# Scores of a pair of heads: two products of 64 rows instead of one block-diagonal product of 128

## The chip, the cores and the metric

One Trainium2 chip, one core. The metric is device time in microseconds of one execution of the whole kernel; lower is better. Every time here comes from runs on the chip, or from the profile of one execution (page, trace).

## The reference

Inputs: q, k, v of 8 batches, 8 heads, 576 positions, 64 values per head; weights of a gated unit. Keys and values are pooled by 8 along the sequence, so each head has 72 pooled keys.

```python
k_p = k.reshape(B, H, Sp, pool, D).mean(axis=3)          # Sp = 576 / 8 = 72
v_p = v.reshape(B, H, Sp, pool, D).mean(axis=3)
scores = scale * np.matmul(q, k_p.transpose(0, 1, 3, 2)) # (B, H, 576, 72)
scores = scores - np.max(scores, axis=-1, keepdims=True)
attn = np.exp(scores)
attn = attn / (np.sum(attn, axis=-1, keepdims=True) + 1e-09)
x = np.matmul(attn, v_p)                                 # then (B, 576, 512)
h = gelu(x @ w_in); u, v = h[..., :512], h[..., 512:]    # tanh form of gelu
v_n = layernorm(v) * g_ln
v_s = np.einsum('ts,bsd->btd', w_sg, v_n) + b_sg[None, :, None]
out = x + (u * v_s) @ w_out
```

All of it is float32. The change is in the line of `scores`.

## The kernel before

The eight heads of a batch are worked on as four pairs (G = 4). For each batch and pair there are small steps, each a Python generator that gives way at its `yield`s: A, B, C and E load k, v, q and what is left over; K pools the keys and puts them into `kbd`; P prepares the pooled values; Q transposes q into `qT`; S computes scores and the softmax; L and T turn the softmax so that keys lie on partitions; V multiplies with the values; H, U, W and O are the products of the gated unit; X and Z finish and store.

The order of all work is written out by hand: the list `PROLOGUE` names one step and batch per word (`S0+3` is the next piece of step S, pair 0, batch 3), and `emit` runs through it. At the end every instruction is tied to the one before it on its engine (line 908), so each engine's order is fixed by that list; only the waits between engines move in time. Engines meet through the tile framework's semaphores.

`mm` (line 138) issues every matrix product, so all of them have line 139 in the profile; the names of tiles tell them apart. Most products use operands split into a high and a low part of type F32R; the scores use plain float32 operands, and such a product appears in the trace as two weight loads and two matmuls.

`kbd` (line 164) holds the pooled keys of all pairs: 128 partitions, 4 pairs, 144 columns. Partitions 0 to 63 are the 64 values of the even head, partitions 64 to 127 those of the odd head. Step K writes the even head's 72 keys into columns 0 to 71 of the upper 64 partitions, and the odd head's into columns 72 to 143 of the lower 64; the other two blocks are zero from the memset in line 165. So one product of `qT` (128 partitions: both heads' values; 576 positions) with `kbd` gives both heads' scores side by side: 144 columns, half of the multiplications being with zeros.

Step S (lines 532 to 583) does that for five blocks of 128 positions (NT = 5; the last block overlaps the one before). `qT`'s block is the operand loaded into the array, `kbd` the one that is streamed. Scores go into one PSUM tile of two banks of 512 values (`mtile()` for batch 0, `atile()` after that, both in rings of two). Blocks stand SLOT = 184 values apart in the flat tile, so three blocks lie in the first bank and two in the second. After a `yield`, VectorE finds the negated maximum of each position and head in one instruction over all five blocks (`nmax`, line 545); ScalarE then runs ten exponentials, one per block and head, each with its own maximum as bias and its sum as a second output (line 564); VectorE adds 1e-9 (line 571), writes the reciprocal, for most steps into two unused PSUM values behind each block (line 577), and scales `e` (line 223). GpSimd copies the last 16 columns aside (line 583).

The tile `aps` is also used by steps L, T (in the first two batches) and V, and the pooling by TensorE in the first two batches (`kvraw` with `ident`, line 390).

Of the kernel before, what the change touches and what calls it, by code (L numbers as in the profile page):

```python
# [13 lines left out]
AF = mybir.ActivationFunctionType  # L14
ALU = mybir.AluOpType
AX = mybir.AxisListType

P = 128
# [75 lines left out]
def tile_pooled_attn_gmlp(ctx: ExitStack, tc: tile.TileContext, q, k, v, w_in, g_ln, w_sg, b_sg, w_out, out):  # L94
    nc = tc.nc
    B, H, S, D = q.shape
    DM = w_in.shape[0]
    DF2 = w_in.shape[1] // 2
    SP = S // POOL
# [3 lines left out]
    NT = -(-S // P)  # L103
    TAIL = S - (NT - 1) * P
    HALF = S // 2
    NB = 512
    SLOT = 184
    NATURAL = (0,)
    FINE = (B - 1,)
    BY_PSUM = ("v",)  # L110
# [16 lines left out]
    def ring(pool, shape, name, bufs):  # L127

        turns[name] = (turns.get(name, -1) + 1) % bufs
        return pool.tile(shape, F32, name=name, tag=f"{name}{turns[name]}")  # L130

    def mtile():
        return ring(psm, [P, 2, NB], "mps", 2)

    def atile():
        return ring(psa, [P, 2, NB], "aps", 2)

    def mm(o, lhsT, rhs, start, stop):
        nc.tensor.matmul(o, lhsT, rhs, start=start, stop=stop)  # L139
# [24 lines left out]
    kbd = const.tile([P, G, 2 * SP], F32, name="kbd")  # L164
# [39 lines left out]
    def ready(func):  # L204

        if loaded.get("now") != func:
            nc.scalar.activation(early, eps[:, 0:1], func)  # L207
        loaded["now"] = func
# [13 lines left out]
    def scale(o, x, y, key):  # L222
        (nc.gpsimd if key in OTHER else nc.vector).tensor_tensor(o, x, y, op=ALU.mult)  # L223
# [307 lines left out]

    def step_S(b, g):
        qT = st.pop(("qT", b, g))
        flat = (mtile() if b == 0 else atile()).rearrange("p a n -> p (a n)")
        slots = []
        for i in range(NT):
            o = flat[:, SLOT * i:SLOT * i + 2 * SP]

            t0 = min(i * P, S - P)
            mm(o, qT[:, t0:t0 + P], kbd[:, g], True, True)  # L540
            slots.append(o.rearrange("p (h k) -> p h k", h=2))
        yield
        nmax = per.tile([P, NT, 2], F32, name="nmax", tag=f"nmax{g}")
        every = flat[:, 0:SLOT * NT].rearrange("p (s k) -> p s k", k=SLOT)[:, :, 0:2 * SP]
        nc.vector.tensor_reduce(out=nmax, in_=every.rearrange("p s (h k) -> p s h k", h=2),  # L545
                                axis=AX.X, op=ALU.max, negate=True)
        yield

        e = ring(per, [P, NT, 2, SP], "e", 3)
        ssum = per.tile([P, NT, 2], F32, name="ssum", tag=f"ssum{g}")  # L550
        mode = SOFTMAX.get(b, 0)
        if mode == 2:

            scores = every.rearrange("p s (h k) -> p s h k", h=2)
            nc.vector.tensor_tensor(e, scores, nmax.unsqueeze(3).broadcast_to([P, NT, 2, SP]), op=ALU.add)
            yield
            ready(AF.Exp)
            nc.scalar.activation(e, e, AF.Exp)
        else:
            ready(AF.Exp)  # L560
            for i in range(NT):
                for h in range(2):
                    acc = {} if mode else {"accum_out": ssum[:, i, h:h + 1]}
                    nc.scalar.activation(e[:, i, h], slots[i][:, h], AF.Exp, bias=nmax[:, i, h:h + 1], **acc)  # L564
        if mode:
            yield
            nc.vector.tensor_reduce(out=ssum, in_=e, axis=AX.X, op=ALU.add)
            nc.vector.tensor_scalar(ssum, ssum, 1e-9, None, op0=ALU.add)
        else:
            yield  # L570
            nc.vector.tensor_tensor(ssum, ssum, eps[:, 0:1].unsqueeze(2).broadcast_to([P, NT, 2]), op=ALU.add)

        key = f"n{min(b, 2)}{g}"
        rec = flat[:, 0:SLOT * NT].rearrange("p (s k) -> p s k", k=SLOT)[:, :, 2 * SP:2 * SP + 2]
        if key in OTHER:
            rec = ssum
        nc.vector.reciprocal(rec, ssum)
        scale(e, e, rec.unsqueeze(3).broadcast_to([P, NT, 2, SP]), key)
        ef = st["e", b, g] = e.rearrange("p t h k -> p t (h k)")
        yield  # L580
        if ("el", b) not in st:
            st["el", b] = per.tile([P, NT, 2, NL, 2], F32, name="el")
        nc.gpsimd.tensor_copy(st["el", b][:, :, g // 2, :, g % 2], ef[:, :, P:2 * SP])
# [274 lines left out]
    def step_Z(b, m):  # L858
        if b in FINE:
# [10 lines left out]


    steps = {"A": step_A, "B": step_B, "C": step_C, "E": step_E, "K": step_K, "P": step_P, "Q": step_Q, "S": step_S, "L": step_L, "T": step_T, "V": step_V,
             "H": step_H, "U": step_U, "W": step_W, "O": step_O, "X": step_X, "Z": step_Z}
    going = {}
# [60 lines left out]
```

## Time and profile before

| | us |
|---|---|
| median of 3 runs | 561.77 (561.52 to 562.21) |
| the profiled execution | 560.36 |
| its span (first to last instruction) | 558.7 |
| TensorE, matmuls busy | 538.1 (96%) |
| TensorE, weight loads busy | 508.7 (91%) |
| VectorE busy | 435.2 (78%) |
| ScalarE busy | 330.6 (59%) |
| GpSimd busy | 260.8 (47%) |

In the profile PE is TensorE's matmuls and PEld its weight loads, which overlap the matmuls; DVE is VectorE, ACT ScalarE, POOL GpSimd, SP the engine that issues most DMAs. A tile is named without its number in the ring. A group of instructions stands as line, engine, operation, output <- inputs, shapes, count, then busy time in us and the mean of one in ns, then the idle time before it and what ended it. For TensorE a shape such as 128*64 is rows by columns of the array. A matmul's record includes its way through the array, so records of products that follow closely overlap one another: what a product costs in a stream is the distance between two starts, and not its length.

### The profile page before, as it was taken

How to read it: one execution, taken by the hardware profiler on the slowest of the kernel's cores; microseconds unless marked ns; L12 is line 12 of the kernel's file. 1: busy time of each engine (PE TensorE's matmuls, PEld its weight loads, DVE VectorE, ACT ScalarE, POOL GpSimd, SP SyncE). 2: the span in 40 equal slices, each digit the busy share in tenths (PEclk: the TensorE clock that was granted, in tenths of full speed). 3: DMA queues.
4: the chain of work that ended last, by engine and by line, in shares of the span. 5: the costliest groups of instructions: out<-in, count | busy, mean ns of one | idle time of the engine just before them, and what ended most of it. 6: DMA issues, size and time to landing. Idle time of an engine off the chain costs nothing.

```text
span 558.7 us, 10694 instructions
## 1 busy us (share of the span) xinstructions
PE 538.1 (96%) x3677; PEld 508.7 (91%) x3677; DVE 435.2 (78%) x644; ACT 330.6 (59%) x1077; POOL 260.8 (47%) x322
## 2 busy tenths in 40 slices
PE   5799998999999999999999999999999999999997
PEld 4687987999999989999999989999999989998996
DVE  2899999998879979788888788788667798736254
ACT  3899995695348924587358834696338674322210
POOL 4365648843815254455507356533707243344130
PEclk9999999999999999999999999999999999999999
DMA  8996342365654365645747377517564423230206
GB/s 246 315 298 164 93 120 76 69 145 122 158 147 90 93 155 146 138 111 134 166 104 158 86 177 162 119 48 151 122 169 99 95 44 83 78 59 2 32 13 106
DMA packets 186470, 68.38 MB, mean 122 GB/s; under 512 B 150576, under 2 KB 170800, under 8 KB 186416
## 3 DMA queue, kind: packets, MB, share of 16 engines
q1 hardware_dynamic: 182560, 67.11, 49.9%
q10 hardware_dynamic: 3856, 0.59, 0.6%
q8 instruction: 29, 0.48, 0.3%
q14 instruction: 25, 0.20, 0.1%
HBM read 48.20 MB, written 19.46 MB: 121 GB/s over the span
## 4 chain that ended last, share of the span: by engine, by line
PE 78%; DVE 9%; ACT 4%; SPq 3%; DMA 3%; issue 1%; POOL 0%; DVEq 0%; ACTq 0%; POOLq 0%
PE mps L139 66%; PE aps L139 12%; SPq L240 3%; ACT e L564 2%; DMA kvraw<-in_k 1%; ACT L207 1%; DVE vg L739 1%; DVE bst L733 1%; DVE al L649 0%; DMA al<-tfar 0%; DVE top L237 0%; DMA lfar<-y 0%; DVE e L223 0%; DVE raw L228 0%; DVE wsl L320 0%
## 5 line engine op out<-in xcount | busy, mean ns | idle before, releaser
L564 ACT ACTIVATE e<-aps,nmax 128x72 f32<-128x72 f32 x280 | 85.0, 354 | 6.3 <-DVE nmax L545 6.2
L139 PE MATMUL mps<-xhl,wih 128*128 128x288 f32 x512 | 88.2, 294 | 0.0
L139 PE MATMUL mps<-wih,xhl 128*128 128x512 f32 x256 | 84.7, 396 | 0.6 <-DVE wsl L320 0.3
L139 PEld LDWEIGHTS mps<-xhl,wih 128*128 128x128 f32 x512 | 75.5, 188 | 1.0
L237 POOL TENSOR_TENSOR glo<-u,ghi 128x576 fp32r<-128x576 f32 x29 | 42.4, 1478 | 69.9 <-ACT ghi L214 35.5
L564 ACT ACTIVATION_READ_ACCUMULATOR e<-aps,nmax 128x1 f32 x280 | 67.4, 242 | 0.0
L237 POOL TENSOR_TENSOR xhl<-x,xhl 128x576 fp32r<-128x576 f32 x30 | 43.8, 1471 | 41.9 <-ACT xhl L692 37.6
L139 PEld LDWEIGHTS mps<-wih,xhl 128*128 128x128 f32 x256 | 48.1, 188 | 11.1 <-ACT u L771 0.7
L139 PE MATMUL mps<-wsh,vhl 128*128 128x288 f32 x256 | 55.1, 296 | 0.3 <-DVE vhl L237 0.3
L139 PE MATMUL mps<-xhl,wil 128*128 128x288 f32 x256 | 54.8, 295 | 0.0
L139 PE MATMUL mps<-wsl,vhh 128*128 128x288 f32 x256 | 54.8, 295 | 0.0
L139 PE MATMUL mps<-wsh,vhh 128*128 128x288 f32 x256 | 54.7, 295 | 0.0
L139 PE MATMUL mps<-ghi,woh 128*128 128x288 f32 (+1 forms) x232 | 51.8, 302 | 0.0
L139 PE MATMUL mps<-ghi,wol 128*128 128x288 f32 (+1 forms) x232 | 50.8, 298 | 0.0
L139 PE MATMUL mps<-glo,woh 128*128 128x288 f32 (+1 forms) x232 | 50.8, 298 | 0.0
L139 PE MATMUL mps<-wil,xhl 128*128 128x512 f32 x128 | 50.1, 391 | 0.0
L785 DVE SCALAR_TENSOR_TENSOR mps<-mps,gcol,bbc 128x576 f32<-128x576 f32 x32 | 26.2, 819 | 27.6 <-PE mps L139 27.6
L237 POOL TENSOR_TENSOR vhl<-vg,vhh 128x512 fp32r<-128x512 f32 x25 | 34.6, 1389 | 23.5 <-DVE vhh L212 18.6
L736 POOL TENSOR_TENSOR rstd<-mv,eps 128x1 f32<-128x1 f32 (+1 forms) x40 | 13.0, 325 | 68.8 <-DVE mv L734 65.5
L646 ACT CAST ah<-al 128x640 fp32r<-128x640 f32 x24 | 17.5, 731 | 41.6 <-DMA al<-tfar 37.9
L139 PEld LDWEIGHTS mps<-wsh,vhl 128*128 128x128 f32 x256 | 41.1, 188 | 0.6 <-DVE vhl L237 0.6
L139 PEld LDWEIGHTS mps<-wsh,vhh 128*128 128x128 f32 x256 | 41.2, 188 | 0.0
(210 smaller groups left out, 1428.8 us busy)
## 6 DMA issues: line engine op xcount, KB each, us to landing
kvraw<-in_k SPq DMA_DIRECT2D x16, 512.0 KB, 4.3
kvraw<-in_v SPq DMA_DIRECT2D x16, 512.0 KB, 4.3
qraw<-in_q SPq DMA_DIRECT2D x112, 72.0 KB, 2.6
out<-y SPq DMA_DIRECT2D x112, 72.0 KB, 2.1
tfar<-y SPq DMA_DIRECT2D x24, 320.0 KB, 2.5
al<-tfar SPq DMA_DIRECT2D x96, 80.0 KB, 2.2
raw<-in_moe_w_in SPq DMA_DIRECT2D x4, 1024.0 KB, 7.8
y<-lfar SPq DMA_DIRECT2D x36, 80.0 KB, 2.1
```

What stands on the lines that cost most here:

```text
L139: nc.tensor.matmul(o, lhsT, rhs, start=start, stop=stop)
L207: nc.scalar.activation(early, eps[:, 0:1], func)
L237: (nc.vector if key in OTHER else nc.gpsimd).tensor_tensor(o, x, y, op=op)
L240: queue.dma_start(o, i)
L564: nc.scalar.activation(e[:, i, h], slots[i][:, h], AF.Exp, bias=nmax[:, i, h:h + 1], **acc)
L646: nc.scalar.copy(ah, al)
L733: nc.vector.bn_stats(bst, vg)
L736: nc.gpsimd.tensor_tensor(rstd, mv[:, 1:2], eps[:n, 1:2], op=ALU.add)
L739: nc.vector.scalar_tensor_tensor(vg, vg, mv[:, 0:1], rstd.broadcast_to([n, DF2]), op0=ALU.subtract, op1=ALU.mult)
L785: nc.vector.scalar_tensor_tensor(vs, vs, gcol[:, d:d + 1], bbc.rearrange("p (a n) -> p a n", a=2), op0=ALU.mult, op1=ALU.add)
```

## The change

The five products of a step become ten. For each block of positions and each of the two heads `h`, the product takes only that head's 64 partitions of `qT` and `kbd` and that head's 72 columns. The even head's scores go into the first bank of the tile, the odd head's into the second; within a bank the five blocks stand SLOT = 96 values apart. The maximum, the exponentials and the reciprocal read and write the same number of values at the new places; the reciprocal now stands in one unused value behind each block and head. `kbd` is filled as before; its zero blocks are no longer read.

```diff
-    SLOT = 184
+    SLOT = 96
...
     def step_S(b, g):
         qT = st.pop(("qT", b, g))
-        flat = (mtile() if b == 0 else atile()).rearrange("p a n -> p (a n)")
-        slots = []
+        slots = (mtile() if b == 0 else atile())[:, :, 0:SLOT * NT].rearrange("p h (s k) -> p s h k", k=SLOT)
         for i in range(NT):
-            o = flat[:, SLOT * i:SLOT * i + 2 * SP]
             t0 = min(i * P, S - P)
-            mm(o, qT[:, t0:t0 + P], kbd[:, g], True, True)
-            slots.append(o.rearrange("p (h k) -> p h k", h=2))
+            for h in range(2):
+                r = slice(D * h, D * h + D)
+                mm(slots[:, i, h, 0:SP], qT[r, t0:t0 + P], kbd[r, g, SP * h:SP * h + SP], True, True)
         yield
         nmax = per.tile([P, NT, 2], F32, name="nmax", tag=f"nmax{g}")
-        every = flat[:, 0:SLOT * NT].rearrange("p (s k) -> p s k", k=SLOT)[:, :, 0:2 * SP]
-        nc.vector.tensor_reduce(out=nmax, in_=every.rearrange("p s (h k) -> p s h k", h=2),
-                                axis=AX.X, op=ALU.max, negate=True)
+        nc.vector.tensor_reduce(out=nmax, in_=slots[:, :, :, 0:SP], axis=AX.X, op=ALU.max, negate=True)
...
-                    nc.scalar.activation(e[:, i, h], slots[i][:, h], AF.Exp, bias=nmax[:, i, h:h + 1], **acc)
+                    nc.scalar.activation(e[:, i, h], slots[:, i, h, 0:SP], AF.Exp, bias=nmax[:, i, h:h + 1], **acc)
...
-        rec = flat[:, 0:SLOT * NT].rearrange("p (s k) -> p s k", k=SLOT)[:, :, 2 * SP:2 * SP + 2]
+        rec = slots[:, :, :, SP]
         if key in OTHER:
             rec = ssum
```

More of the change, by code (lines that the diff above doesn't have):

```diff
@@ L552, in step_S @@
         if mode == 2:
-            scores = every.rearrange("p s (h k) -> p s h k", h=2)
-            nc.vector.tensor_tensor(e, scores, nmax.unsqueeze(3).broadcast_to([P, NT, 2, SP]), op=ALU.add)
+            nc.vector.tensor_tensor(e, slots[:, :, :, 0:SP], nmax.unsqueeze(3).broadcast_to([P, NT, 2, SP]), op=ALU.add)
             yield
```

## The prediction

> **What bounds the kernel now.** I read the page first: the span, the busy shares and the chain that ended last.
>
> ```profile
> span 558.7 us, 10694 instructions
> PE 538.1 (96%) x3677; PEld 508.7 (91%) x3677; DVE 435.2 (78%) x644; ACT 330.6 (59%) x1077; POOL 260.8 (47%) x322
> PE 78%; DVE 9%; ACT 4%; SPq 3%; DMA 3%; issue 1%; POOL 0%; DVEq 0%; ACTq 0%; POOLq 0%
> ```
>
> TensorE is busy 96% of the span and holds 78% of the chain. An average can hide stages, so next comes the view by stretches (stretch, its length, busy time of PE, PEld, DVE, ACT and POOL with their instructions, then clock and DMA):
>
> ```profile
> 0.00:50.00 50.00, 38.68 (x257) 33.80 (x258) 36.66 (x56) 36.78 (x130) 24.62 (x43) 1.00 0.90 259
> 50.00:100.00 50.00, 46.77 (x316) 42.99 (x315) 47.52 (x75) 40.84 (x133) 35.00 (x41) 1.00 0.39 109
> 100.00:200.00 100.00, 100.00 (x700) 96.24 (x699) 87.44 (x131) 66.47 (x240) 48.08 (x60) 1.00 0.52 119
> 300.00:400.00 100.00, 98.96 (x666) 93.37 (x665) 81.03 (x124) 65.55 (x235) 53.11 (x66) 1.00 0.54 122
> 450.00:540.00 90.00, 89.11 (x604) 84.14 (x603) 53.85 (x80) 31.79 (x68) 34.62 (x40) 1.00 0.21 46
> ```
>
> From 100 us on TensorE is never without work, and its clock is granted in full. What it waited for from 100 us to the end is one short list:
>
> ```profile
> PE aps L139 <- DVE e L223: 1.0, 1, 1.0
> PE mps L139 <- POOL xta L218: 0.4, 1, 0.4
> PE mps L139 <- DVE vhl L237: 0.3, 1, 0.3
> ```
>
> So time that a product saves or costs on TensorE after 100 us goes to the end nearly one to one. The products that change are those of step S, scores from the tiles qT and kbd. The view of tile qT (matmuls, count, shortest/median/longest ns, first and last start) and its busy time by stretch (the first number after the length) say how many there are and where:
>
> ```profile
> L139 PE MATMUL aps<-kbd,qT x280: 283/286/390, 48.4 to 446.8; 128*128 128x144 f32 x140
> L139 PE MATMUL mps<-kbd,qT x40: 286/286/390, 14.3 to 26.6; 128*128 128x144 f32 x40
> 50.00:100.00 50.00, 4.24 (x30) 1.00 0.39 109
> 100.00:200.00 100.00, 10.61 (x80) 1.00 0.52 119
> 200.00:300.00 100.00, 7.90 (x60) 1.00 0.61 145
> 300.00:400.00 100.00, 8.41 (x61) 1.00 0.54 122
> 400.00:450.00 50.00, 5.65 (x40) 1.00 0.50 114
> ```
>
> Each of the 32 steps issues 5 products, and an f32 product stands as two records, each with its own weight load: 10 loads and 10 matmuls a step, 320 in all. About 240 of them, 24 steps, lie after 100 us. The chain of waits (start, length, what) runs through them:
>
> ```profile
> 106.85 2.45 PE aps L139 x20
> 181.41 1.23 PE aps L139 x10
> 185.01 1.22 PE aps L139 x10
> 244.16 1.23 PE aps L139 x10
> ```
>
> One step costs 1.225 us of the path; two back to back cost 2.45. That is 0.1225 us a record.
>
> **The change, part by part.** *Removed:* 10 pairs of load and matmul per step (128 rows, 128 weight columns, 144 moving columns), 1.225 us. *Added:* 20 pairs per step, each of 64 rows, 128 weight columns and 72 moving columns; those of the even head stand in rows 0 to 63 and write one half of the tile (one PSUM bank), those of the odd head in rows 64 to 127 and the other half. What a pair costs has two parts.
>
> The matmul: if time goes by moving columns, 72 of them cost 0.1225 x 72/144 = 0.061 us. The load: it still has 128 columns. Two places price it. In the first, weights of 64 and of 128 columns follow each other after a wait, by the timeline of loads (start, length):
>
> ```profile
> 461.20 0.13 PEld L139 LDWEIGHTS mps<-wil,xta 128*64 128x64 f32 x1 [0.90 <-POOL xta L218]
> 461.25 0.19 PEld L139 LDWEIGHTS mps<-wih,xta 128*128 128x128 f32 x1
> 461.49 0.14 PEld L139 LDWEIGHTS mps<-wil,xta 128*64 128x64 f32 x1
> 461.72 0.19 PEld L139 LDWEIGHTS mps<-wih,xta 128*128 128x128 f32 x1
> ```
>
> The second load begins 0.05 us behind the first: 64 columns occupy the load path for about 0.05 us, and as the records' means differ by 0.054 us, too (below), 128 columns occupy it for about 0.108. In the second place, pairs with 128 moving columns, the pooling of k and v, run back to back:
>
> ```profile
> L139 PEld LDWEIGHTS mps<-wil,xta 128*64 128x64 f32 x32 | 4.3, 134 | 2.4 <-POOL xta L218 0.9
> L139 PEld LDWEIGHTS mps<-xhl,wih 128*128 128x128 f32 x512 | 75.5, 188 | 1.0
> L139 PEld LDWEIGHTS aps<-lt,vl 96*128 96x128 f32 x48 | 9.1, 189 | 0.0
> 60.85 1.95 PE L139 MATMUL aps<-kvraw,ident 128*128 128x128 f32 x16
> ```
>
> Sixteen starts in 1.95 us less the last record's 0.29: 1.66/15 = 0.111 us a pair. So a load of 128 columns costs 0.108 to 0.111 us, and 96 rows cost what 128 rows cost (189 and 188 ns): halving the rows makes no load cheaper. Now the load, not the matmul, sets the pace of a pair (0.111 against 0.061).
>
> Hence the question that decides the sign: do loads of the two row groups run side by side? No row of this trace has 64 rows, so both bounds stand. Side by side, each group passes 10 loads: 10 x 0.111 = 1.11 us a step, a gain of 0.115. One behind the other: 20 x 0.111 = 2.22 us, a loss of 0.99. I take side by side: the rows show that a load's time goes by columns and not by rows, as it would where each row of the array takes in its own weights, and loads here already run under matmuls in flight. That is the nearer reading, not a proof.
>
> The Trainium skill bears on this on both sides. In "TensorE: Matmul & The Clock Gate", section LDWEIGHTS, a load costs its column count whatever its rows; the trace agrees (188 and 189 ns), and by this rule alone, with one load at a time, the change doubles the load time. In "TensorEngine Tiling (Array Packing)", Key Properties, tiles load weights and multiply in parallel; no run here shows it yet.
>
> *Switching the array* between products of 128 rows and of 64: the nearest rows are products of 64 weight columns between those of 128, matmuls on the same timeline:
>
> ```profile
> 461.49 0.39 PE L139 MATMUL mps<-wih,xta 128*128 128x512 f32 x1
> 461.72 0.39 PE L139 MATMUL mps<-wil,xta 128*64 128x512 f32 x1
> 461.95 0.40 PE L139 MATMUL mps<-wih,xta 128*128 128x512 f32 x1
> ```
>
> They follow each other every 0.23 us, less than a record's own 0.39, so nothing drains between the two shapes. I take nothing for a switch; the upper bound is a full drain: the flight of the last product (0.286 - 0.122 = 0.164) and an uncovered load (0.108), 0.27 us, at each way in and out.
>
> The same page of the Trainium skill, Key Properties, says that changing the tiling mode drains the engine; the rows above speak against it for columns, and rows are not tried here. It is a rival below.
>
> *Readers of the scores:* the maximum, the exponentials and the reciprocal keep their counts and sizes.
>
> ```profile
> L545 DVE TENSOR_REDUCE nmax<-aps 128x10 f32<-128x720 f32 x28 | 25.0, 894 | 11.3 <-PE aps L139 11.2
> L564 ACT ACTIVATE e<-aps,nmax 128x72 f32<-128x72 f32 x280 | 85.0, 354 | 6.3 <-DVE nmax L545 6.2
> L577 DVE RECIPROCAL aps<-ssum 128x10 f32<-128x10 f32 x28 | 6.3, 224 | 1.0
> ```
>
> Only strides change; the old layout also had three products in one bank and two in the other. I cost this at nothing: VectorE and ScalarE have slack under TensorE (87 and 66 of 100 us). Without that cover even a tenth on the 894 ns would be 28 x 0.09 = 2.5 us. No wait, DMA or queue entry is added or moved; the next step behind S on TensorE starts earlier or later by what S gains or loses.
>
> **The sum.** 24 steps x (1.11 - 1.225) = -2.8 us. Of the 8 steps before 100 us, where the stretches show TensorE with idle time, 0 to 8 x -0.115 = -0.9; I take -0.3. Together -3.1. The profiled execution took 560.36 us with a span of 558.7; its sum is 557.3. The median of the runs is 561.77, 1.4 above it, so the forecast for the median is **558.7 us**.
>
> **The rivals.**
> *Loads one behind the other* (slower). Place: the load path in step S. Price: 24 x 0.99 = +23.7, and 0 to +7.9 for the early eight, of which I take +3: about 588.5 us, bounds 585.5 to 593.4. It decides once the mean spacing of S's loads is above 0.061 us, where 20 of them exceed 1.225. For it: loads on TensorE stand in one order, and every f32 product needs two. Against it: that rows don't enter a load's time.
> *A drain at each switch.* The steps after 100 us come in about 18 stretches, since pairs like that at 106.85 share one: 18 x 2 x 0.27 = +9.7 on top of -3.1, 568.4 us; with a third of that price it would end where it began. Against it: the 64-column rows.
> *The change doesn't do what it says.* Loads overlap but the matmuls of the two groups take turns: 20 x 0.061 = 1.22 us a step, as before: 561.7 us.
> *Both faster.* If loads, too, were paced below the 0.061 of a matmul, a step would take 0.61 us: 24 x -0.61 = -14.7, 547 us. The 0.108 speaks against it.
> *Loads in turn and a drain:* 598 us.
>
> **How the numbers follow.** Forecast 0.37, both faster 0.04, no gain 0.10, drain 0.14, loads in turn 0.32, in turn with a drain 0.03. A measurement of this kernel can tell about 0.2% (1.1 us) from no change. Faster: 0.37 + 0.04 = 0.41. Same: 0.10 and 0.02 of the drain's (a small one that eats the gain) = 0.12. Slower: 0.12 + 0.32 + 0.03 = 0.47. The forecast's own range is 557 to 560.5 us, from the 0.108 and 0.111 and the early steps. As cases of both signs hold most of the chance, the range runs from 556.5 to 591: it leaves out the faster extreme, loads in turn with a drain, and the upper third of the loads in turn.
>
> **What would show it.** In the profile after, the records of qT and kbd have 64 rows and 72 columns and are twice as many (640). Right: the chain's piece for one step is about 1.11 us, loads of both groups begin within some ns of each other, and the product after S follows without a gap. Loads in turn: those starts are 0.108 us apart and the piece is 2.2 us. A drain: some 0.2 us of idle TensorE before the first load of S and behind the last matmul. The forecast is wrong if a step's piece is above 1.2 us, or if TensorE shows new waits for DVE or ACT behind S.

## The result, and the profile after

The changed kernel takes 569.52 us (median of 4 runs, 566.21 to 570.59) against 561.99 for the kernel before (561.52 to 563.04). The ratio is 1.0118, with a 95% interval from 1.0096 to 1.0141: slower by 1.2% (7.5 us between the medians). The forecast was 558.7 us, so its sign was wrong; the time lies inside the range given. The profiled execution took 569.15 us with a span of 567.4, 8.8 us above the profiled one of before.

The page after: span, busy shares, the granted clock in 40 slices and the engines of the chain.

```profile
span 567.4 us, 11333 instructions
PE 546.8 (96%) x3997; PEld 511.6 (90%) x3997; DVE 436.1 (77%) x644; ACT 331.1 (58%) x1077; POOL 260.1 (46%) x322
PEclk9699999999999999999999999999999999999999
PE 74%; DVE 12%; DMA 5%; ACT 3%; SPq 3%; issue 2%; POOL 0%; DVEq 0%; ACTq 0%; POOLq 0%
```

There are 320 more loads and matmuls, VectorE and ScalarE are as busy as before, and the clock falls to 0.6 in the second slice (14 to 28 us), which it did not do before. Where the time goes is read best from the view of tile qT, whose first and last starts can be set beside those in the prediction:

```profile
L139 PE MATMUL aps<-kbd,qT x560: 272/272/327, 52.8 to 455.6; 64*128 64x72 f32 x187
L139 PE MATMUL mps<-kbd,qT x80: 272/280/486, 15.8 to 30.9; 64*128 64x72 f32 x80
```

The steps of batch 0 (`mps`) began at 14.3 us before and begin at 15.8; the first step after them began at 48.4 and begins at 52.8, 4.4 us late; the last one began at 446.8 and begins at 455.6, 8.8 us late. The end is 8.7 us late. So half of the loss is there before 53 us, half comes in the 400 us of steps, and after the last step nothing is added.

Of the first 4.4 us, 1.5 are a later start. Ahead of the first step ScalarE waits for a load from memory, before and then after:

```profile
10.55 1.16 ACT L285 ACTIVATE mps<-raw 128x512 f32<-128x512 f32 x2 [2.01 <-DMA raw<-in_moe_w_in]
```

```profile
12.08 1.16 ACT L285 ACTIVATE mps<-raw 128x512 f32<-128x512 f32 x2 [3.25 <-DMA raw<-in_moe_w_in]
```

No instruction that the change touches stands ahead of it. In the traces of the experiments below this wait is 1.9 to 3.3 us, and in the kernel before and its versions alone 2.0 to 3.1 us. So these 1.5 us are more likely scatter than a part of the change, though that isn't proved.

The second half first. Matmuls (the first three lines) and weight loads (the last four) around two adjacent steps after the change; start, length:

```profile
110.89 0.42 PE L139 MATMUL mps<-wtl,vht 128*128 128x288 f32 x2
111.24 2.46 PE L139 MATMUL aps<-kbd,qT 64*128 64x72 f32 x40
113.62 0.53 PE L139 MATMUL mps<-wsh,vhh 128*128 128x288 f32 x2
...
110.76 0.32 PEld L139 LDWEIGHTS mps<-wtl,vht 128*128 128x128 f32 x2
111.24 0.19 PEld L139 LDWEIGHTS aps<-kbd,qT 64*128 64x128 f32 x2 [0.16 <-issue]
111.24 2.31 PEld L139 LDWEIGHTS aps<-kbd,qT 64*128 64x128 f32 x40 [0.16 <-issue]
113.62 0.30 PEld L139 LDWEIGHTS mps<-wsh,vhh 128*128 128x128 f32 x2
```

The same stretch in the kernel before:

```profile
106.42 0.43 PE L139 MATMUL mps<-wtl,vht 128*128 128x288 f32 x2
106.68 2.61 PE L139 MATMUL aps<-kbd,qT 128*128 128x144 f32 x20
109.04 0.52 PE L139 MATMUL mps<-wsh,vhh 128*128 128x288 f32 x2
...
106.55 2.53 PEld L139 LDWEIGHTS aps<-kbd,qT 128*128 128x128 f32 x20
109.01 0.31 PEld L139 LDWEIGHTS mps<-wsh,vhh 128*128 128x128 f32 x2
```

Three things are to be seen. *The row groups do run side by side:* two loads begin within 111.24 to 111.25 us (the row with x2 is that window), and 40 loads in 2.31 - 0.19 us are 20 pairs, 2.12/19 = 0.112 us a pair. A step costs 1.12 us instead of 1.225, as forecast. *On the way in there is a gap:* before, the loads of S began at 106.55, under the last product of W (which ended at 106.85); after, they begin at 111.24, only 0.07 us ahead of that product's end at 111.31, and TensorE's loads stand still for 0.16 us. *On the way out, too:* from the end of S (111.24 + 2.46 = 113.70) to the end of the next two matmuls (114.15) pass 0.45 us, where it was 0.27 (109.29 to 109.56): 0.18 us more; the loss of a single step by starts, below, gives 0.20.

The chain shows the way in and the steps together, for a pair of steps and for a single one:

```profile
111.31 2.38 PE aps L139 x40
250.05 1.27 PE aps L139 x20
```

A single step is 1.27 = 1.12 + 0.15, and 0.20 on the way out: 1.47 against 1.225, a loss of 0.24. A pair is 2.38 + 0.20 = 2.58 against 2.45, a loss of 0.13. The 24 steps after 100 us stand in 12 single stretches and 6 pairs: 12 x 0.24 + 6 x 0.13 = 3.7 us by these prices. Read stretch by stretch, as the shift between the two traces from the products ahead of a stretch to those behind it, it is 3.0 us: the six pairs lose 0.12 to 0.13 each and nine of the single steps 0.23 to 0.25, but the other three, whose first load came late in the kernel before, too, hardly anything (-0.07 to 0.09). The rest of the 4.4 us that the tile's starts show, about 1.4, comes between the stretches, in part as short waits of TensorE that are longer in this trace (for `vhl` 0.7 us instead of 0.3). Why they are longer was not followed.

What is left of the first half, some 2.9 us, goes with the clock. Busy time by stretch, 9 to 36 us, before and then after (after the five engines: granted clock, DMA):

```profile
9.00:36.00 27.00, 21.21 (x164) 18.93 (x164) 22.68 (x38) 22.61 (x104) 9.64 (x14) 1.00 1.06 319
```

```profile
9.00:36.00 27.00, 21.18 (x173) 19.32 (x172) 18.46 (x32) 18.46 (x95) 6.92 (x9) 0.81 1.02 313
```

In these 27 us TensorE was granted 0.81 of its clock after the change, and all of it before. Cut where the clock changes, the trace after shows full clock and half clock in turn (the second and the fourth line are at 0.50):

```profile
9.62:16.42 6.80, 3.17 (x32) 2.67 (x32) 3.55 (x6) 3.19 (x9) 0.52 (x2) 1.00 0.92 228
16.44:19.84 3.40, 3.40 (x24) 3.04 (x20) 2.27 (x4) 1.60 (x9) 1.26 (x1) 0.50 1.13 324
19.86:23.25 3.39, 2.10 (x26) 1.72 (x25) 3.02 (x6) 3.39 (x22) 2.17 (x2) 1.00 1.04 394
23.27:30.08 6.81, 6.45 (x40) 6.12 (x42) 5.32 (x10) 6.26 (x37) 1.87 (x3) 0.50 1.05 308
```

In all four runs of the change the mean clock over the whole span is 0.987 to 0.992.

### The profile page after: what moved, and what is told of

Read it like the earlier page. It is cut to its first block, busy times and chain, and to the rows that moved or that the text cites. A ratio compares the mean times of both kernels' runs of the same rounds, so it can differ in the third digit from the quotient of the medians.

```text
span 567.4 us, 11333 instructions
## 1 busy us (share of the span) xinstructions
PE 546.8 (96%) x3997; PEld 511.6 (90%) x3997; DVE 436.1 (77%) x644; ACT 331.1 (58%) x1077; POOL 260.1 (46%) x322
## 4 chain that ended last, share of the span: by engine, by line
PE 74%; DVE 12%; DMA 5%; ACT 3%; SPq 3%; issue 2%; POOL 0%; DVEq 0%; ACTq 0%; POOLq 0%
PE mps L139 60%; PE aps L139 13%; SPq L240 3%; DMA raw<-in_moe_w_in 1%; DMA al<-tfar 1%; DVE vg L735 1%; DVE e L223 1%; DVE bst L729 1%; ACT e L560 1%; DMA out<-y 1%; DVE al L645 1%; DVE ssum L567 1%; DMA lfar<-y 0%; DVE y L863 0%; DVE top L288 0%
```

## The experiments

The first four take the loss apart by place and by switch. Batch 0 back in the old form:

```diff
...
         for i in range(NT):
 
             t0 = min(i * P, S - P)
+            if b == 0:
+                mm(slots[:, i], qT[:, t0:t0 + P], kbd[:, g].rearrange("p (h k) -> p h k", h=2), True, True)
+                continue
             for h in range(2):
...
```

(The lines left out give batch 0 its old places in PSUM, 184 values apart.)

> The change everywhere but in batch 0, whose four steps keep the one product of 128 rows. Theory: half of the 7.5 us comes from the first 35 us, where the granted clock fell to 0.5 for some 10 us in the profile after, and half from 0.15 us on the way into 64 rows and 0.20 us on the way out of them at each of the later stretches. Then the clock stays at 1.00 and 565.5 to 567 us remain. Rival, the early loss has nothing to do with the batch-0 products (a late load, or the program's greater length): about 569.5 us, clock 0.99. Rival, the later stretches cost nothing: 562 us.

Measured: 564.71 us (1.0052 of before, 1.0036 to 1.0068), clock 0.997 to 1.000 in four runs. Its steps in the view by tile:

```profile
L139 PE MATMUL aps<-kbd,qT x560: 272/272/327, 48.6 to 451.2; 64*128 64x72 f32 x187
L139 PE MATMUL mps<-kbd,qT x40: 286/286/390, 14.4 to 26.7; 128*128 128x144 f32 x40
```

The first step after batch 0 is back at 48.6 us, the last is 4.4 us late. The early loss is gone and the later one is whole. The time is 0.8 us below the expected band, and 2.8 us above the kernel before; between the runs of both with a clock of 0.999 or more it is 3.2 us.

The opposite, the new form in batch 0 alone (the same edit with `if b > 0`):

> The change in batch 0 alone. Theory: the early loss stays and the later one goes: 564.5 to 566.5 us, mean clock near 0.99. Rival, the early loss isn't made by these four steps: within 1 us of the kernel before (562 to 563), clock 1.00.

Measured: 565.02 us (1.0054, 1.0026 to 1.0082; seven runs from 561.68 to 567.5), clock 0.985 to 0.996. The run with the highest clock (0.996) is the fastest, 561.68 us and no slower than the kernel before; that with the lowest is the slowest. From the view by tile, the two forms:

```profile
L139 PE MATMUL aps<-kbd,qT x280: 283/286/362, 52.2 to 451.0; 128*128 128x144 f32 x140
L139 PEld LDWEIGHTS mps<-kbd,qT x80: 183/330/335, 14.2 to 30.4; 64*128 64x128 f32 x80
```

The same run by stretch, 9 to 36 us (after the five engines: granted clock, DMA):

```profile
9.00:36.00 27.00, 22.34 (x175) 20.18 (x175) 19.55 (x33) 19.06 (x96) 6.59 (x9) 0.75 1.04 322
```

Batch 0 starts in time at 14.2 us, but the first step after it is 3.8 us late. Most loads of batch 0 take 330 ns instead of 183, and the granted clock of the stretch is 0.75; from there on only 0.4 us are added. So the two halves show apart: by the ratios 0.52% and 0.54%, together 1.06%, against 1.18% for the whole change, which the intervals allow.

Then the switch itself. One of the five blocks of each step is done with all 128 rows, as two products of 72 columns at the same place, first the middle block and then, as a control, the first one (`if i > 0` in place of `if i != 2`):

```diff
-                r = slice(D * h, D * h + D)
+                r = slice(D * h, D * h + D) if i != 2 else slice(0, P)
```

> The change, but the third of the five blocks of positions is done as two products of 128 rows and 72 columns (kbd's zeros included), at the same place in PSUM. Each step so leaves the 64 rows once more and comes back once more. Theory (0.35 us per way out and in): 8.4 us (24 steps after 100 us) to 11.2 us (32) above the run with the first block done so. Rival, switching costs nothing and the loss has another cause: equal to that run within 1 us.

> The control: the same two products of 128 rows, for the first block of each step, where a stretch of 64 rows only starts later. Against the change as it is: the block's four loads in a row cost 4 x 0.111 instead of 2 x 0.111 us, +0.22 a step, so +5.3 to +7.1 us, and six pairs of adjacent steps are cut in two, +2.1 us by the theory: 577 to 579 us. Rival, no price for switching: 575 to 576.5 us.

Measured: 584.49 us with the middle block (1.0398, 1.0374 to 1.0422) and 577.77 with the first (1.0285, 1.0269 to 1.0301), which is in the expected band: 6.7 us between them. The clock does not make this difference: it is the lower one with the first block (0.982 to 0.985 against 0.985 to 0.990). The 8.4 to 11.2 expected were miscounted: in a pair of steps the middle blocks cut the 64-row work in three and the first blocks in two, so a pair has one switch more and not two. That makes 18 more ways out and in after 100 us, 18 x 0.35 = 6.3 us, and a few early. One step of each, with the product ahead of it (middle block, then first block):

```profile
192.95 0.43 PE L139 MATMUL mps<-xhl,wil 128*128 128x288 f32 x2
193.30 1.86 PE L139 MATMUL aps<-kbd,qT 64*128 64x72 f32 x20
```

```profile
191.13 0.42 PE L139 MATMUL mps<-xhl,wil 128*128 128x288 f32 x2
191.39 1.60 PE L139 MATMUL aps<-kbd,qT 128*128 128x72 f32 x20
```

From the end of the product ahead (193.38 and 191.55) to the end of the step (195.16 and 192.99) pass 1.78 and 1.44 us: 0.34 for one more way out and in, the same work otherwise. The switch has its price, and it is no matter of where the stretch lies.

Two runs on the row groups. All products with 128 rows (`r = slice(0, P)`), and all five of the even head ahead of the five of the odd one:

```diff
-        for i in range(NT):
-            t0 = min(i * P, S - P)
-            for h in range(2):
+        for h in range(2):
+            for i in range(NT):
+                t0 = min(i * P, S - P)
```

> All ten products of a step with 128 rows and 72 columns (kbd's zeros included), at the same places in PSUM: what the change would cost without the two row groups. Theory (the row groups run side by side, and a load of 128 columns sets the pace): 20 x 0.111 = 2.22 us a step, no way in or out, so 24 x 1.0 = +24 us over the kernel before and up to 8 more early: 586 to 594 us. Rival, the matmuls and not the loads set the pace: 20 x 0.061, no change, 562 us.

> The same ten products of 64 rows, but all five of the even head first and then the five of the odd head. If TensorE takes loads strictly in order, the groups no longer run side by side: about 20 x 0.111 = 2.2 us a step, 24 x 1.1 = +26 us over the change: 594 to 600 us. If it looks some 20 instructions ahead, the steps stay at 1.12 us: 569.5 us.

Measured: 593.34 us, as the theory says, and 594.73 us (1.0546 and 1.0571, two runs each). A single step and a pair in the chain, with 128 rows and then with the heads in turn:

```profile
115.67 4.42 PE aps L139 x40
196.18 2.18 PE aps L139 x20
```

```profile
119.39 3.45 PE aps L139 x40
197.40 1.99 PE aps L139 x20
```

With 128 rows the loads stand in one line: 2.18 us a step, 0.109 a load, with no way in or out; the row groups are worth 1.06 us a step. As the places in PSUM are those of the change, it is not the new layout that costs at the ends of a stretch. With the heads in turn neither answer holds, though the time lies in the band of the first. The loads begin to overlap in the middle of the step (loads that start in 197.30 to 198.05, and in the 0.39 us after that):

```profile
197.33 0.85 PEld L139 LDWEIGHTS aps<-kbd,qT 64*128 64x128 f32 x7 [0.17 <-ACT vbh L480]
197.88 0.69 PEld L139 LDWEIGHTS aps<-kbd,qT 64*128 64x128 f32 x9
```

Seven loads in the first 0.75 us, which is one at a time, and then seven more starts in half that time (the row of nine counts two of the first seven again). By their spacing of 0.11 us, the odd head's loads begin at 198.06 us, when the even head still has three to go (198.11, 198.22 and 198.33): TensorE takes a load of the other row group ahead of waiting products, but here only over three pairs of load and matmul, not over the ten of a head. The order of the change, head by head within a block, is the one that lets the groups overlap. The time of this run is as long as that with 128 rows, although two adjacent steps take 1 us less (3.45 against 4.42); its clock is the lowest of all (0.971 and 0.980, against 0.994 and 0.996), which by the line at the end of this section is worth some 7 us.

Four runs look for what lowers the clock. Five products of ident with itself ahead of each step of batch 0, in the change and, as a control, in the kernel before:

```diff
+        for _ in range(5 if b == 0 else 0):
+            mm(ps[:, 0, 0:P], ident, ident, True, True)
```

> The change, and ahead of the ten products of each of the four batch-0 steps five products of ident with itself (128 rows, 128 columns, 1.1 us together), written where the scores go afterwards and overwritten by them. They only keep the array streaming where TensorE waited or loaded. Theory: the clock fell in batch 0 because the products of 64 rows stream for 0.061 of every 0.111 us and the stretch has idle time besides; with the filling the clock stays at 0.995 or more and 565 to 567 us are left, the later stretches' loss alone. Rival, the fall has another cause (the length of the program, the order of transfers): clock 0.99 or less, 569 to 572 us.

> The control: the kernel before with the same five products in each batch-0 step. If the filling by itself does nothing, 561 to 562.5 us and a clock of 0.997 to 1.000; if the work added is on the path, up to 4 x 1.1 = 4.4 us more, 566 us; if the runs of the kernel before with a clock of 0.995 lose by it, 560.5 to 561 us.

Measured: 568.17 us (four runs from 566.97 to 572.08, clock 0.994 to 1.000) and, in the kernel before, 564.1 (1.004, 1.0017 to 1.0062; clock 0.999 to 1.000 in ten runs). The 568.17 us are above the 565 to 567 expected, since the filling costs 2.7 us itself: in two steps it stands behind the wait for the tile and ahead of products that others wait for. With that cost in both, the change is 4.1 us above its control. The clock is held in part only: the profiled run still has half clock from 22.9 to 26.3 us. The two runs with a clock of 0.999 or more, 566.97 and 567.13 us, are 2.9 us above the control: the later half of the loss, without the early one.

The filling fitted to the idle time (4, 0, 5 and 2 products):

> The change, with the filling only where TensorE waits anyway: 4, 0, 5 and 2 products of ident ahead of the batch-0 steps of pairs 0 to 3 (0.9, 0, 1.1 and 0.4 us; TensorE waited 1.3 us ahead of the first step, 1.8 ahead of the third and 0.7 ahead of the fourth before the change). Theory: the clock is held and the filling costs little: 565 to 566.5 us, between the run with the old batch 0 (564.7) and the change (569.5). Rival, the fall of the clock isn't set by how busy the array is: clock 0.992 or less and 569 us or more.

> The control: the kernel before with the same fitted filling. If it costs nothing there: 560.5 to 562 us and a clock of 0.999 or 1.000 in every run; it would then be a little faster than the kernel before (561.4 to 562), whose clock fell below 0.998 in some of its runs. If the filling is on the path: 563 us.

Measured: 571.85 us (1.0185, 1.0162 to 1.0209) with a clock of 0.986 to 0.989, and 564.45 (1.0044, 1.0028 to 1.0061; clock 0.996 to 1.000) in the kernel before, where up to 563 was expected. The clock was not held: it fell to half from 22 to 32 us, and the filling in that stretch ran at half speed, too. This is what the rival said, so the filling does not show that too little streaming is the cause. That the second step has no filling here is a possible reason that no run tested alone.

Last, the kernel before with less streaming in batch 0 and no row groups. In the first of the two the odd heads of batch 0 are left out; in the second each product is split in two of 72 columns:

```diff
+            if b == 0:
+                mm(o[:, 0:SP], qT[:, t0:t0 + P], kbd[:, g, 0:SP], True, True)
...
             mm(o, qT[:, t0:t0 + P], kbd[:, g], True, True)
```

> The kernel before, but in batch 0 each product has 128 rows and only the even head's 72 columns; the odd head's softmax reads the even head's scores (so the odd heads of batch 0 are left out). A step there lasts about 10 x 0.109 = 1.09 us and streams for 0.61 us of them, like the change, but without row groups. Theory A, the clock falls by how little the array streams: clock 0.985 to 0.996 and 563 to 567 us, as with the change in batch 0 alone. Theory B, products of 64 rows as such lower it: clock 0.997 to 1.000 and 560.5 to 562.5 us.

> The kernel before, but in batch 0 each product of 144 columns is two of 72 columns, all with 128 rows. A step there lasts about 20 x 0.109 = 2.18 us and streams as long as before, 1.22 us. Theory A: the streaming is as before, spread over time that TensorE in part waited through: clock 0.993 to 1.000; time 562 to 566 us, since up to 1 us a step can be on the path. Theory B: clock 0.997 to 1.000, the same time. Should the share of streaming within busy time count, and not its amount: clock 0.985 to 0.992.

Measured: 563.21 us (1.0024, 0.9996 to 1.0052; ten runs from 560.43 to 566.35) with clocks from 0.984 to 1.000, six of the ten at 0.991 or less; and 567.5 us (1.0102, 1.0071 to 1.0133), clock 0.991 to 0.994, slower than the 562 to 566 expected. Beside them the kernel before had 0.992 to 1.000, with a median of 0.997. So products of 128 rows that stream for 0.61 us of a 1.09 us step lower the clock, too (median 0.991, against 0.988 with the 64 rows in batch 0): the row groups as such are not needed for it. In the time the first of the two is not clear of no change. The second is a little below the clock expected of the same streaming in more time, and doesn't decide between amount and share.

What the clock is worth can be read from the 49 runs of the kernel before beside these experiments, whose clocks lie between 0.987 and 1.000: a straight line through them falls by 3.5 us for each 0.01 of mean clock (3.0 without the one run at 0.987). By that line the change's 0.987 to 0.992 cost it 3 to 4.5 us against a full clock.

## Why the prediction was wrong

*What bounds the kernel, and that S's products lie on the path:* right in the main. The 3.0 us that the stretches lost after 100 us came out at the end: from the first step after batch 0 to the last one the trace of e1 loses 4.2 us and that of the change 4.4, with over 1 us of other waits in it.

*The price of a pair, and side by side:* right. Forecast 1.11 us a step, measured 1.12. One of the two prices of a load rested on the wrong row: the pooling's pairs move 128 columns, and at 0.1225 us for 144 columns their matmul alone takes 0.109, so their 0.111 us need not be the load. What shows that the load sets the pace is e7, with 72 columns and 0.109 us a pair. The rival "loads one behind the other" would have cost 2.22, and e7 shows that price (2.18) where the row groups are taken away. In the Trainium skill, "TensorEngine Tiling (Array Packing)", Key Properties, tiles load and multiply in parallel. The two loads at 111.24 us agree.

*Switching the array: "I take nothing for a switch".* This is the step that failed. The 64-column products among those of 128 were the row taken, and what they show doesn't hold for rows: the way from 128 rows to 64 costs 0.15 us and the way back 0.20, 0.35 a stretch. The upper bound in the prediction, 0.54 for both, was too high, in part since the next load begins 0.07 us ahead of the end of the last product. With 0.35, the sum's -0.105 a step turns into +0.24 for a single step; a stretch would need more than three adjacent steps to break even. The rival "a drain at each switch" is what happened, with both signs that the prediction named for it: 0.16 us without a load ahead of S and 0.18 us behind it. Products of 96 rows would have misled in the same way as those of 64 columns: in the kernel before they follow those of 128 rows without a gap (`aps<-lt,vl`, 151.83 us, between products at 151.71 and 151.95). The same section of the Trainium skill says that changing the tiling mode drains the engine. For 128 to 64 rows the trace agrees, by the gap and not quite to the full drain, and for columns the rows of before still show none.

*The early steps: "0 to -0.9; I take -0.3".* Wrong by some 3.5 us (+3.1 in e2), and no case held it. The prediction costed TensorE's work before 50 us as if only idle time could be touched. But with the new products the granted clock fell to half there for 10 us, and in e2 TensorE's work between 16 and 30 us took nearly twice as long (loads of 330 ns instead of 183). That the new products of batch 0 do it is shown by e1 and e2; that their shorter streaming is the reason is supported by e11 and not shown. In the Trainium skill, "TensorE: Matmul & The Clock Gate", Part 1, the clock is gated by how busy the array has been in windows of 3.4 us. The traces agree with a fall to exactly half, in spells of 3.4 us and multiples of it, and in e11 with a lower clock where the array streams less. Against the plain form of this speaks e9, where more streaming did not hold the clock; e9 and e12 leave open which measure of activity counts.

*The readers of the scores:* right. The maximum, the exponentials and the reciprocal show no change (895, 354 and 224 ns each against 894, 354 and 224); VectorE and ScalarE have the same busy time (436.1 and 331.1 against 435.2 and 330.6 us).

*The sum in the end:* some +3 us for the steps with their switches (2.8 to 3.2 in e1, 3.0 in the trace) and some +3 for the clock (3.1 in e2) make about 6 of the 7.5 us, where -3.1 was forecast; the rest is not placed and is near the noise (1.06% against 1.18% by the ratios). The prediction's own chances leaned the other way than its number, 0.47 for slower and 0.41 for faster. That the drain rival's 568.4 lies near the result is half chance: its switches were priced too high, 9.7 us against 18 x 0.35 = 6.3, by about what the clock took.

No run gave a version faster than the kernel before. Nor do the prices promise one: a stretch gains 0.105 us a step and pays 0.35, and scores have only two PSUM tiles, so more than two adjacent steps would have to wait for the softmax.

## What to carry to other kernels

Two products in different row groups do run side by side, also at full load on TensorE; but a product's pace is then set by its weight load (0.11 us for 128 columns), and each stretch of 64-row work among 128-row work costs 0.35 us at its two ends, so put such work in long stretches or leave it. A row of the trace that looks like the operation in question (switching by columns) is no bound for it (switching by rows): keep the full price as a case with a large chance. And where TensorE has idle time, changing its work to a lighter one cost clock here: look at the granted clock in the stretches that are only just busy enough.

## What the runs showed of the hardware

- 64-row products in two row groups: loads of both begin within 0.01 us of each other, a pair each 0.112 us; 0.15 us on the way from 128 rows to 64 and 0.18 to 0.20 on the way back; switching between 128 and 64 weight columns shows neither.
- The overlap needs the two groups to stand close to each other: with ten loads of one group ahead of ten of the other, seven loads run alone before the second group's begin, and a single step takes 1.99 us instead of 1.27.
- The granted clock fell to half for spells of 3.4 us and multiples with lighter work; as a mean over the span it was 0.985 to 0.996 with the new products in batch 0 alone, 0.984 to 1.000 with half the columns left out there, 0.987 to 1.000 over 49 runs of the kernel before, at some 3.5 us for each 0.01.
- Still open: which measure of the array's activity sets the clock, why some waits between the stretches grew, and whether any of the 1.5 us by which the first step started later in the profile after belongs to the change. In the profile of e2 the first step starts at 14.2 us, as before.
